# Block 0's down product of a fused attention and SwiGLU kernel: another order for three VectorE sums, for the sums of x and for two groups of basis work

## The chip, the cores and the metric

The kernel runs on one core of one Trainium2 chip. The metric is the device time of one execution in microseconds (us). Its time before is 1006.44 us, the median of three runs (1006.27 to 1007.7). All times below are us unless they are marked ns.

A core has a matrix engine (TensorE, PE in the profile; its weight loads are PEld), a vector engine (VectorE, DVE), a scalar engine (ScalarE, ACT), a general one (GpSimd, POOL), and SyncE (SP), which here only issues DMAs. Each engine works its own queue in order, and they meet at semaphores. SBUF is the working memory; PSUM, in banks, is where matmuls leave their results.

## The reference

```python
kv  = einsum('bhsd,bhse->bhde', k, v)           # 8 batches, 8 heads, 576 positions, head size 64
o   = einsum('bhsd,bhde->bhse', q, kv)
x   = o / sqrt(mean(o * o, -1) + 1e-6) * g_norm # reshaped to 4608 x 512
g   = x @ w_gate                                # 512 x 1536
out = (g * sigmoid(g) * (x @ w_val)) @ w_out    # 1536 x 512
```

Everything is float32 in the kernel; the weights arrive as 64-bit words and are rounded on the chip.

## The kernel before, in words

**Tiling.** The 4608 rows are nine blocks of 512. Each goes through attention (class `Att`: x of the block, transposed), an *up* product (`Up`, `Inner`: h = silu(x w_gate) * (x w_val), in six pairs of 128-wide columns) and a *down* product (`Down`: h w_out). Block 0's up is a plain product (`plain_up`); blocks 1 and 2 and all downs but the last use one level of a seven-product scheme for 2 x 2 blocks (Strassen's, in Winograd's form); the last six blocks go in pairs, with two levels in their ups. While a block is in its down, the next block's attention is worked in between.

**The seven products.** P1 to P7 are each a chain of matmuls. `CHAIN` (line 634) gives each a bank of PSUM: P1, P6, P7 and P4 add up in one bank "b"; P2 has a bank "a"; P5 opens a bank "c", and P3 adds on top of it. After some products the result is taken out, or partly summed, by ACT or DVE: `after1`, `after6`, `after2`, `after7`, `after4`, `after3`. The operands need sums: S1 to S4 of the left side, T sums of the weights (the *basis*: `t2` and the subtractions in `Up.prepare` and `turn_t`).

**Block 0's down.** `Ffn.down` (line 1453) goes through P1, P6, P5, P7, P2, P4, P3, 24 matmuls each. Named here:

- `after7` (line 1380) copies bank b on ACT (U3) and then adds bank c, P5, to it on DVE. This sum is `added`. P3 is written into the same bank c, so P3 waits until `added` has read it.
- `after2` (line 1374) adds bank a, P2, to the copy of P1 on DVE (here "the sum with P2"), and then computes S4 on DVE, 128 x 1536, in place of an operand of P2. P3 reads S4.
- `after4` and `after3` finish the two halves of the block's output, which SP stores.

**Block 1's attention beside it.** `Att.steps` (line 601) hands three steps to block 0's down: the products of q with kv, norms and transposes after P1 (`whole`), the transposed blocks' DMAs after P5 (`place_x`: 16 DMAs, eight of them issued on ACT's queue, eight on SP's), and after P2 the gain on ACT (`gain_x`) and the four sums of x on DVE (`sums`, `sum_steps`). Block 1's P5 reads the first of these sums, P6 the third.

**Basis work.** In lines 1711 to 1716 `t2` (line 1574) makes, on DVE, two instructions for each of six pairs of w_val's columns. The first three pairs are queued behind block 1's scaled x (`nxt.halves[0]`), the other three behind S4 and `added`. POOL subtracts from what `t2` leaves (`Up.prepare`, line 693).

**The kept leaves.** For blocks 3 to 8 the weights are also turned into the second level's 49 combinations ("leaves"), written to DRAM by SP (`send_leaf`), and streamed back later. `kept_steps(0)` (line 1304) is the work for pair 0 in two halves, each of four DVE instructions (three of 128 x 256, one of 128 x 512) and two DMAs; four raw DMAs follow. The first half is placed by hand in `alone` (line 1636) ahead of block 0's down. The second half is handed to block 1's up, in `Up.multiply` (line 748): its first instruction, `held`, is queued behind block 1's scaled x (`ffn.att.scaled`), for pair 1 behind `ffn.added`, the sum of P5 and U3 of block 1's pair 0. SP's sends keep the program's order. The halves for pair 0 and pair 1 use the same room in SBUF, so pair 1's second half waits until pair 0's second half has been sent.

**What sets the order.** The kernel is written in a framework that sets all semaphores itself and orders each engine's queue by its own reckoning of when things are ready. `tc.issue_after(ins)` is the hand's way in: whatever the block under it issues on the engine of `ins` comes behind `ins` in that engine's queue. `in_order` fixes a whole stretch; it is not used around the change. In block 0's down DVE's queue before had, after x's scaling and transposes: `t2` of pairs 0 to 2 with the four instructions of the kept half among them, the sum with P2, S4, `added`, then `t2` of pairs 3 to 5 with x's sums among them.

Of the kernel before, what the change touches and what calls it, by code (L numbers as in the profile page):

```python
# [18 lines left out]
def kernel(  # L19
# [41 lines left out]
    nc = tc.nc  # L61
# [5 lines left out]
    BLK = P * T  # L67
    HB = BLK // 2
    HD = DM // 2
# [61 lines left out]
    add = lambda e, o, a, b: e.tensor_tensor(out=o, in0=a, in1=b, op=OP.add)  # L131
    sub = lambda e, o, a, b: e.tensor_tensor(out=o, in0=a, in1=b, op=OP.subtract)  # L132
# [24 lines left out]
    def ring():  # L157

        return r_pool.tile([P, 4, BLK], F32, name="r")
# [75 lines left out]
    class Att:  # L235
# [300 lines left out]
        def sums(self):  # L536

            for step in self.sum_steps():
                step()

        def sum_steps(self):

# [54 lines left out]
        def turn(self):  # L597
            for i in range(2):
                self.turn_q(i, (c_psum if self.n == 1 else m_psum, b_psum))
# [45 lines left out]
    class Quad:  # L645
# [9 lines left out]
        def multiply(self, p):  # L655
            name, first = CHAIN[p]
            if first:
                self.ps[name] = PSUMS[name].tile([P, 2, HB], F32, name=name)
            ps = self.ps[name]
            for e, i in self.order(p):  # L660
                lhsT, rhs = self.operands(p, e, i)

                self.ffn.multiplied = nc.tensor.matmul(  # L663
                    ps[:, e], lhsT=lhsT, rhs=rhs, start=first and i == 0 and e == 0, stop=i == self.steps - 1,
                    skip_group_check=True,
                )
            getattr(self, f"after{p}", lambda: None)()
# [17 lines left out]
    class Up(Quad):  # L685
# [24 lines left out]
        def after2(self):  # L710
            add(nc.vector, self.s, self.ps["a"], self.s)
            if self.j == NP - 1:
                nc.scalar.activation(out=self.s, in_=self.s, func=ACT.Silu)
# [34 lines left out]
        def multiply(self, p):  # L748
            super().multiply(p)
            ffn = self.ffn  # L750
            if ffn.n == 1:
                if p == 5:
                    self.leaf_room = chunks(ring())
                if p in (5, 7, 4):
                    at = 3 * (5, 7, 4).index(p)
                    ffn.making.extend(leaf_steps(self.j, [(self.w[p].unsqueeze(1), (p,))], self.leaf_room[:, at:]))
                if p == 3:
                    if self.j < 2:
                        first, *steps = first_kept if self.j == 0 else kept_steps(self.j, chunks(xi_alone))

                        def held():
                            with tc.issue_after((ffn.added if self.j else ffn.att.scaled).ins):
                                first()

                        ffn.later += [held, *steps]
# [503 lines left out]
    def leaf_steps(j, sources, room):  # L1269


        i = 0
        for t, os in sources:
            n = len(os)
            t = t.rearrange("p o i (e c) -> p o i e c", e=2)
            b11, t2_, b22 = t[:, :, 0, 0], t[:, :, 0, 1], t[:, :, 1, 1]
            to = room[:, i : i + 3 * n].rearrange("p (o r) c -> p o r c", r=3)
            yield lambda b22=b22, t2_=t2_: sub(nc.vector, t2_, b22, t2_)
            yield lambda b11=b11, t2_=t2_: add(nc.vector, t2_, t2_, b11)
            yield lambda t=t, t2_=t2_, to=to, n=n: sub(  # L1280
                nc.vector, to[:, :, 1:3], t[:, :, 1], t2_.unsqueeze(2).to_broadcast([P, n, 2, P])
            )
            yield lambda t=t, os=os: send_leaf(j, os, (1, 6, 2, 3), t.rearrange("p o i e c -> p o (i e c)"))
            yield lambda b11=b11, t2_=t2_, to=to: sub(nc.vector, to[:, :, 0], b11, t2_)
            yield lambda to=to, os=os: send_leaf(j, os, (7, 4, 5), to.rearrange("p o r c -> p o (r c)"))
            i += 3 * n
# [13 lines left out]
    def chunks(t):  # L1300

        return t.rearrange("p f (s c) -> p (f s) c", c=P) if len(t.shape) == 3 else t.rearrange("p a b c -> p (a b) c")
# [21 lines left out]
    class Down(Quad):  # L1324
# [47 lines left out]
            sub(nc.vector, pairs[:, 0, :, 0:HB], pairs[:, 0, :, HB:BLK], pairs[:, 1, :, HB:BLK])  # L1372

        def after2(self):
            add(nc.vector, self.o1[:, :, 0:HD], self.ps["a"], self.s)

            pairs = self.ffn.h.rearrange("p (j e) t -> p e j t", e=2)
            self.s4 = sub(nc.vector, pairs[:, 1, :, 0:HB], pairs[:, 1, :, 0:HB], pairs[:, 0, :, HB:BLK])

        def after7(self):  # L1380
            o = ring()
# [185 lines left out]
    def weights(upto):  # L1567
        nonlocal rounded
        while rounded < min(upto, len(pieces)):
            load_weights(rounded + 4)  # L1570
            round_w(*pieces[rounded])
            rounded += 1

    def t2(place, b22, b11):

        sub(nc.vector, place, b22, place)
        return add(nc.vector, place, place, b11)
# [58 lines left out]
    def alone(n):  # L1636
        ffn = Ffn(n, blocks[n])
        nxt = blocks[n + 1]
        if n == 0:

            with tc.issue_after(squared.ins), tc.issue_after(scaled.ins):
                weights(2)
            ffn.plain_up(0, (0,))
            copied = blocks[0].copied
            blocks[0].turn_x(1)
            for f in range(NF - 1):
                with tc.issue_after(blocks[0].copied.ins if f else copied.ins):
                    weights(2 * (f + 2))
                ffn.plain_up(f) if f else ffn.plain_up(0, (1,))
            weights(len(pieces))  # L1650
            pairs = wo.rearrange("p (j e) d -> p e j d", e=2)
            turned = t2(pairs[:, 0, :, HD:DM], pairs[:, 1, :, HD:DM], pairs[:, 0, :, 0:HD])
            nxt.room = xi_alone.rearrange("p a b c -> p (a b c)")

            with tc.issue_after(sent.ins):
                for i in range(2):
                    nxt.load_kv(i)
                nxt.load_quarters(0)
            with tc.issue_after(ffn.silus[NF - 2].ins):
                for step in nxt.quarter_steps(1, (0, 1), (nc.scalar,)):  # L1660
                    step()
            with tc.issue_after(turned.ins):
                nxt.turn_q(0)
            with tc.issue_after(nxt.q_turned.ins):
                multiplied = ffn.plain_up(NF - 1)
            with tc.issue_after(multiplied.ins):
                nxt.turn_q(1)
            ffn.s1 = s_pool.tile([P, NP, HB], F32, name="s1")
            ffn.plain_end()
            for g in range(2):  # L1670
                nxt.kv(g)
            with in_order(nc.vector.engine), tc.issue_after(nxt.q_turned.ins):
                one, two = ffn.sum_steps()
                one()
                for _ in range(6):
                    first_kept.pop(0)()
                two()
        elif n == 1:

            def third():  # L1680
                visit(ffn, nxt, (0, 1))
                for i in range(2):
                    nxt.load_q(i)

            ffn.up({(1, 7): third})
            nxt.turn()
            blocks[PAIRED].load_kv(0)
        else:
            with in_order(nc.vector.engine, nc.scalar.engine):
                ffn.up(ahead(ffn, nxt, blocks[PAIRED + 1]))  # L1690
            nxt = blocks[PAIRED + 1]
            nxt.turn()
            for g in range(2):
                blocks[PAIRED + 2].load_kv(g)
        if n == 2:
            ffn.down_.opens = PAIRED

        def inner_sums():
            with tc.issue_after(nxt.scaled.ins):
                blocks[PAIRED].inner_sums()  # L1700

        def second_kv():
            with tc.issue_after(nxt.placed.ins):
                blocks[PAIRED].load_kv(1)

        ffn.down(nxt, {1: {5: second_kv}, 2: {7: inner_sums}}.get(n, {}))
        if n == 0:
            for g in range(2):
                blocks[2].load_kv(g)

            with tc.issue_after(nxt.halves[0].ins):
                for j in range(NP // 2):
                    t2(wv[j][:, 0:2], wv[j][:, 2:4], wg[j][:, 0:2])
            with tc.issue_after(ffn.down_.s4.ins), tc.issue_after(ffn.down_.added.ins):
                for j in range(NP // 2, NP):
                    t2(wv[j][:, 0:2], wv[j][:, 2:4], wg[j][:, 0:2])

    first_kept = list(kept_steps(0, chunks(xi_alone)))
    for n in range(PAIRED):
        with in_order(nc.tensor.engine) if n == 2 else ExitStack():  # L1720
            alone(n)
# [65 lines left out]
```

## Time and profile before

| what | value |
|---|---|
| median of three runs | 1006.44 (1006.27, 1006.44, 1007.7) |
| the profiled execution | 1004.65 |
| its span, first to last instruction | 1002.8 |
| TensorE's granted clock, mean | 0.999 |
| TensorE busy | 986.6 (98%) |
| VectorE busy | 714.0 (71%) |
| GpSimd busy | 408.8 (41%) |
| ScalarE busy | 231.3 (23%) |
| block 0's down on TensorE, P1 to P3 | 115.7 to 156.1 of the span |
| block 1's up on TensorE | 156.0 to about 231 |

The profile is of one execution. A row of the timeline or of the chain gives the start in us from the span's start, the length, the engine, the line of the kernel (a helper's line where a helper records the instruction: L131, L132 and L133 are `add`, `sub` and `mul`, L663 is the matmul of `Quad.multiply`), the tile written and those read (r, wo, arena, t lie in SBUF; a, b, c, m are PSUM), the partitions and elements, and, in brackets, how long the engine was idle before it and what ended that. Matmuls overlap, and their ends are modelled, so starts are the safer reading. A wait list gives who waited for whom: the total, how often, the longest.

### The profile page before, as it was taken

Reading aid. Unit: us, or ns where it says so; the run is one execution under the profiler, and the core shown is the slowest. Engines: PE = TensorE matmul, PEld = TensorE weight load, DVE = VectorE, ACT = ScalarE, POOL = GpSimd, SP = SyncE. Lnnn points to the kernel's source line nnn. Section 1 sums busy time; section 2 is a strip of 40 time slices with the busy share of each in tenths; the row PEclk is TensorE's granted clock in tenths of the full one; section 3 lists DMA queues with packets and bytes.
Section 4 is the critical chain, followed back from the end, with each engine's and each line's share of the span. In section 5 each row is a group of like instructions: output and inputs, shape, how many; then the busy total and the mean of one; then the engine's idle time right before and its main releaser. Section 6 shows DMA issues by size and latency. Waiting matters only on the chain.

```text
span 1002.8 us, 17762 instructions
## 1 busy us (share of the span) xinstructions
PE 986.6 (98%) x6758; PEld 833.9 (83%) x6758; DVE 714.0 (71%) x1171; ACT 231.3 (23%) x367; POOL 408.8 (41%) x328
## 2 busy tenths in 40 slices
PE   6999999999999999999999999999999999999998
PEld 4544688888888888888888888888888888888998
DVE  2999697678858576656675846666776576666894
ACT  2766111221122312121211111122112112122100
POOL 0000263355544240444566003555651078999300
PEclk9999999999999999999999999999999999999999
DMA  8689743573866855766752365667412556565123
GB/s 230 200 265 265 154 74 119 123 260 95 211 135 127 208 112 167 186 185 169 171 151 43 99 158 149 159 178 179 111 19 67 119 169 204 182 212 161 48 84 96
DMA packets 268261, 151.54 MB, mean 151 GB/s; under 512 B 150288, under 2 KB 250128, under 8 KB 268176
## 3 DMA queue, kind: packets, MB, share of 16 engines
q1 hardware_dynamic: 230928, 144.89, 53.0%
q10 hardware_dynamic: 37184, 5.51, 3.2%
q8 instruction: 54, 0.88, 0.4%
q14 instruction: 31, 0.25, 0.1%
q0 software_dynamic: 64, 0.00, 0.0%
HBM read 109.12 MB, written 32.83 MB: 142 GB/s over the span
## 4 chain that ended last, share of the span: by engine, by line
PE 94%; DVE 3%; DMA 1%; ACT 1%; issue 0%; SPq 0%; DVEq 0%; ACTq 0%
PE b L826 22%; PE b L663 21%; PE c L663 11%; PE c L826 11%; PE a L826 5%; PE a L663 5%; PE b L1489 4%; PE c L1489 4%; PE b L905 4%; PE c L905 2%; PE m L436 1%; PE m L375 1%; DVE arena L132 1%; PE a L905 1%; DMA arena<-in_v_dram 1%; DVE arena L131 0%
## 5 line engine op out<-in xcount | busy, mean ns | idle before, releaser
L826 PE MATMUL b<-arena,t 128*128 128x256 f32 x1008 | 244.5, 381 | 0.0
L826 PEld LDWEIGHTS b<-arena,t 128*128 128x128 f32 x1008 | 190.0, 190 | 29.4 <-DVE r L131 2.3
L131 DVE TENSOR_TENSOR r<-b,r 128x512 f32<-128x512 f32 (+1 forms) x248 | 146.0, 601 | 67.5 <-PE b L826 54.9
L131 POOL TENSOR_TENSOR r<-r 128x256 f32<-128x256 f32 (+1 forms) x90 | 94.8, 1056 | 168.0 <-DMA t<-w 93.3
L131 DVE TENSOR_TENSOR r<-c,r 128x512 f32<-128x512 f32 (+1 forms) x171 | 105.6, 625 | 58.1 <-PE c L826 40.0
L133 POOL TENSOR_TENSOR arena<-r 128x1024 f32<-128x1024 f32 (+1 forms) x54 | 101.7, 1899 | 92.9 <-DVE r L131 49.1
L131 DVE TENSOR_TENSOR r<-a,r 128x512 f32<-128x512 f32 x95 | 60.3, 635 | 100.3 <-PE a L663 64.0
L132 POOL TENSOR_TENSOR t<-wo 128x512 f32<-128x512 f32 x45 | 64.1, 1445 | 162.7 <-DVE wo L131 102.9
L132 DVE TENSOR_TENSOR arena<-arena 128x512 f32<-128x512 f32 (+4 forms) x117 | 123.1, 1069 | 10.2 <-PE b L663 7.0
L826 PE MATMUL c<-arena,t 128*128 128x256 f32 x504 | 122.5, 379 | 0.0
L826 PEld LDWEIGHTS c<-arena,t 128*128 128x128 f32 x504 | 95.6, 190 | 13.5 <-DVE r L131 0.3
L663 PE MATMUL b<-wo,arena 128*128 128x256 f32 x336 | 76.4, 382 | 0.1
L840 ACT COPY r<-b 128x512 f32<-128x512 f32 x54 | 31.7, 586 | 190.0 <-PE b L826 190.0
L663 PE MATMUL b<-t,arena 128*128 128x256 f32 x336 | 74.8, 379 | 0.0
L132 POOL TENSOR_TENSOR t<-arena 128x512 f32<-128x512 f32 x36 | 51.9, 1456 | 55.1 <-PE c L663 21.4
L663 PEld LDWEIGHTS b<-t,arena 128*128 128x128 f32 x336 | 63.8, 190 | 8.7
L663 PEld LDWEIGHTS b<-wo,arena 128*128 128x128 f32 x336 | 63.1, 190 | 9.6 <-DVE arena L133 0.9
L826 PE MATMUL a<-arena,t 128*128 128x256 f32 x252 | 66.1, 379 | 0.0
L826 PEld LDWEIGHTS a<-arena,t 128*128 128x128 f32 x252 | 47.9, 190 | 6.5
L663 PE MATMUL b<-arena 128*128 128x256 f32 x192 | 45.5, 380 | 0.0
L663 PE MATMUL b<-arena,t 128*128 128x256 f32 x192 | 45.4, 379 | 0.0
L1489 PE MATMUL b<-arena 128*128 128x512 f32 (+1 forms) x104 | 43.5, 561 | 0.6 <-ACT arena L500 0.6
(142 smaller groups left out, 1408.2 us busy)
## 6 DMA issues: line engine op xcount, KB each, us to landing
t<-w SPq DMA_DIRECT2D x180, 256.0 KB, 3.2
ld<-in_k_dram SPq DMA_DIRECT2D x26, 288.0 KB, 4.4
ld<-in_v_dram SPq DMA_DIRECT2D x26, 288.0 KB, 6.0
out_dram<-r SPq DMA_DIRECT2D x14, 512.0 KB, 3.2
t<-w SPq DMA_DIRECT2D x54, 128.0 KB, 2.7
ld<-in_moe_w_gate_dram SPq DMA_DIRECT2D x12, 512.0 KB, 4.7
ld<-in_moe_w_val_dram SPq DMA_DIRECT2D x12, 512.0 KB, 4.5
ld<-in_moe_w_out_dram SPq DMA_DIRECT2D x12, 512.0 KB, 4.7
```

The lines of the kernel that those rows point to most:

```text
L131: add = lambda e, o, a, b: e.tensor_tensor(out=o, in0=a, in1=b, op=OP.add)
L132: sub = lambda e, o, a, b: e.tensor_tensor(out=o, in0=a, in1=b, op=OP.subtract)
L133: mul = lambda e, o, a, b: e.tensor_tensor(out=o, in0=a, in1=b, op=OP.mult)
L375: self.positions = nc.tensor.matmul(self.kv_ps[r][u * D : (u + 1) * D, g, :], lhsT=k[:, u, c, :], rhs=v[:, u, c, :], start=(c == 0), stop= ...
L436: self.multiplied = nc.tensor.matmul(self.ps[i][u][p : p + D, t, j, :], lhsT=self.qt[rows, tile_t, head, p : p + D], rhs=kvs[b % 3][rows, ...
L663: self.ffn.multiplied = nc.tensor.matmul(ps[:, e], lhsT=lhsT, rhs=rhs, start=first and i == 0 and e == 0, stop=i == self.steps - 1, skip_g ...
L826: self.ffn.multiplied = nc.tensor.matmul(ps[:, i], lhsT=stream.use(self.ffn.n, self.j, o, p), rhs=self.operand(o, p), start=first and i == ...
L840: copied = nc.scalar.copy(out=dst, in_=ps)
L905: self.ffn.multiplied = nc.tensor.matmul(ps[:, i, f], lhsT=self.deep.operand(o, p, c)[:, f], rhs=self.deep.weight(o, p, c, f), start=first ...
L1489: nc.tensor.matmul(t, lhsT=w[f // 2][:, i, P * (f % 2) : P * (f % 2 + 1)], rhs=x[:, i, of], start=(i == 0), stop=(i == NS - 1),)
```

## The change

Three edits, all to the order of queues; no instruction is added or taken away.

1. `after2`, in block 0 alone: S4 is queued behind `added`, and the sum with P2 behind S4. Before, and still in the other blocks, the sum with P2 is issued first and S4 second, with no order to `added`.
2. `Up.multiply`: the second half of `kept_steps(0)` is queued behind `ffn.added` (as pair 1's already was), no longer behind block 1's scaled x.
3. `alone`: `t2` of pairs 3 to 5 is queued behind S4 and the last of x's sums (`sums` now keeps it as `last_sum`), no longer behind S4 and `added`.

```diff
@@ Att.sums
             for step in self.sum_steps():
-                step()
+                self.last_sum = step()
@@ Up.multiply
                         def held():
-                            with tc.issue_after((ffn.added if self.j else ffn.att.scaled).ins):
+                            with tc.issue_after(ffn.added.ins):
                                 first()
@@ Down.after2
-            add(nc.vector, self.o1[:, :, 0:HD], self.ps["a"], self.s)
-
             pairs = self.ffn.h.rearrange("p (j e) t -> p e j t", e=2)
-            self.s4 = sub(nc.vector, pairs[:, 1, :, 0:HB], pairs[:, 1, :, 0:HB], pairs[:, 0, :, HB:BLK])
+
+            def turn():
+                self.s4 = sub(nc.vector, pairs[:, 1, :, 0:HB], pairs[:, 1, :, 0:HB], pairs[:, 0, :, HB:BLK])
+
+            def total():
+                return add(nc.vector, self.o1[:, :, 0:HD], self.ps["a"], self.s)
+
+            if self.ffn.n == 0:
+                with tc.issue_after(self.added.ins):
+                    turn()
+                with tc.issue_after(self.s4.ins):
+                    total()
+            else:
+                total()
+                turn()
@@ alone
-            with tc.issue_after(ffn.down_.s4.ins), tc.issue_after(ffn.down_.added.ins):
+            with tc.issue_after(ffn.down_.s4.ins), tc.issue_after(nxt.last_sum.ins):
                 for j in range(NP // 2, NP):
                     t2(wv[j][:, 0:2], wv[j][:, 2:4], wg[j][:, 0:2])
```

## The prediction

> **What bounds the kernel now.** I read the page's busy times first, then all waits of TensorE, then its timeline around the change, then the chain there, and last the queues of DVE, ACT, POOL and SP.
>
> ```profile
> PE 986.6 (98%) x6758; PEld 833.9 (83%) x6758; DVE 714.0 (71%) x1171; ACT 231.3 (23%) x367; POOL 408.8 (41%) x328
> ```
>
> TensorE works 98% of the span, so only its idle time can be won. From 36 us to the end the list of its waits has one entry over a tenth of a microsecond:
>
> ```profile
> PE c L663 <- DVE r L131: 1.4, 1, 1.4
> ```
>
> It lies in block 0's down, in the timeline of TensorE:
>
> ```profile
> 133.59 5.34 PE L663 MATMUL b<-t,arena 128*128 128x256 f32 x24
> 138.77 5.34 PE L663 MATMUL a<-wo,arena 128*128 128x256 f32 x24
> 143.95 5.34 PE L663 MATMUL b<-t,arena 128*128 128x256 f32 x24
> 150.66 5.45 PE L663 MATMUL c<-wo,arena 128*128 128x256 f32 x24 [1.37 <-DVE r L131]
> 155.95 0.38 PE L663 MATMUL b<-arena 128*128 128x256 f32 x1
> ```
>
> The rows are P7, P2, P4, P3 and the first matmul of block 1's up. P3 goes onto the bank c that holds P5, so it needs `added` (the sum that reads P5), and S4 for its operand. The chain names what made `added` late:
>
> ```profile
> 141.09 3.09 DVE arena L131 x2
> 144.18 0.02 issue
> 144.20 3.06 DVE arena L132 x2
> 147.26 0.60 DVE r L131
> 147.87 2.14 DVE arena L132
> 150.01 0.61 DVE r L131
> ```
>
> The last three are the sum with P2, S4, and `added`. `added` ran last, though its other input, the copy of U3 on ACT, was there at 142.4:
>
> ```profile
> 141.80 0.59 ACT L1384 COPY r<-b 128x512 f32<-128x512 f32 x1 [12.17 <-DMA arena<-r]
> ```
>
> **The change part by part**
>
> **`added` first, then S4, then the sum with P2.** Nothing is added or removed; three DVE instructions change places. DVE is in order, so behind `added` wait S4, the sum, x's sums and three pairs' basis. `added` can run from 142.4 to 143.1 (0.68 by its row). S4 overwrites an operand of P2, which ends at 144.1. It is 128x1536. It took 2.22 in place (147.79), and the same form 1.75 at 125.33 with POOL idle. The highest bound, three times the longest 128x512 beside POOL (1.75), is 5.25. So S4 ends between 145.9 and 149.4; I take 2.22, the row of S4 itself: 146.4. Without a wait P3 starts at 143.95 + 5.18 = 149.13 (5.18 is the distance of P7, P2 and P4). Only the highest bound makes P3 wait, 0.27. P1 of block 1 would start at 149.13 + 5.18 = 154.31, where it now starts at 155.95: **a gain of 1.64** (1.53 from P3's start, 0.11 from the resumed pass, whose successor comes 5.29 after it instead of 5.18). By the bounds of S4: 1.64 - 0.27 = 1.37 to 1.64.
>
> The Trainium skill ("SBUF — State Buffer", section "SBUF: two separate sides") speaks against moving S4 here: a DVE instruction with two SBUF inputs and a GpSimd one share a port pair that one holds for a whole instruction, while the other blocks. POOL runs basis subtractions from 137.57 to 152.80, and rows agree: 128x256 takes 0.42 at 118.07 and 1.49 at 139.60, beside POOL. By the rule S4 waits for one POOL instruction (1.27 alone) and then runs its 1.75, 3.0 in all, ending at 147.1, in time; by its own row at 146.4. Both leave the gain at 1.64.
>
> **The sum with P2 later.** From about 146.4 to 147.1, or 150.1 at the highest bound. It frees bank a, next needed by P2 of block 1's first pair (161.13 now, 159.5 then). That cover is over 9 us; gone, it would cost one for one.
>
> **x's sums ahead of three pairs' basis (`t2`, j of 3 to 5).** Four instructions overtake six. `gain_x` ends on ACT at 146.15, so the sums can start right behind the sum with P2. The first to need one is P5 of block 1's first pair, at 154.31 + 1.73 = 156.0 (1.73 is what eight matmuls take in the chain); it reads the first sum. P6, at 157.8, reads the third. At the longest row, 1.75 each, from the latest start, 150.1, the first ends by 151.9, the third by 155.4, and the fourth by 157.1, before anything reads it. The basis is read by POOL's subtractions for pair 3, the first of which runs at 162.56 and waits for a DMA. So nothing here is on the path; I count 0, from 0 to 0.
>
> **The second half of `kept_steps(0)` moves into block 1's up.** This is the second hunk, and the part with a price. Its four DVE instructions now run at 139.60, 142.69, 144.20 and 145.78, and take 1.41 + 1.51 + 2.99 = 5.9 of DVE's time there:
>
> ```profile
> 145.78 1.49 DVE L132 TENSOR_TENSOR arena<-arena 128x256 f32<-128x256 f32 x1
> ```
>
> The other half, the same four forms at 118.07 with POOL idle, took 1.94 in all. Taken out, they let `t2` of pairs 0 to 2 end by about 141, before U3's copy. Put behind the `added` of block 1's pair 0 (165.62 now, 163.98 then), they delay DVE by 1.94 to 5.9. I take 1.94, since POOL has one subtraction there (167.28, then 165.6). Their four DMAs sit on SP behind the leaf sends and ahead of the next sends:
>
> ```profile
> 173.77 0.32 SPq L1267 DMA_DIRECT2D w<-r  x1
> 174.14 2.11 SPq L1267 DMA_DIRECT2D w<-arena  x4
> ```
>
> Their place on SP is fixed, but they go only after DVE's leaf work, which the set now delays. DVE waits for their landing:
>
> ```profile
> 173.67 0.68 DVE L131 TENSOR_TENSOR r<-c,r 128x512 f32<-128x512 f32 x1
> 176.16 1.04 DVE L132 TENSOR_TENSOR arena<-arena 128x256 f32<-128x256 f32 x1 [1.82 <-DMA w<-arena]
> ...
> 180.43 0.68 DVE L131 TENSOR_TENSOR r<-c,r 128x512 f32<-128x512 f32 x1
> ```
>
> The last row is `added` of pair 1, which frees bank c for P3 of pair 1 (184.30; with the gain 182.66). DVE from 166.3 to 174.3 is full, so nothing absorbs the delay. The sum then ends at 181.11 - 1.64 + 1.94 = 181.4, and P3 still has 1.2 of cover. With 5.9 it ends at 185.4 and P3 waits 2.7. I take no stall.
>
> **The sum.** 1.64 + 0 + 0 - 0 = 1.64 less; at the worst ends of both unknown costs 1.37 - 2.7, that is 1.3 more. The profiled execution has a span of 1002.8 and took 1004.65, 1.85 around the span; it becomes 1001.2 and 1003.0. The median shown, 1006.44, is 1.79 above that execution; the same 1.64 off it gives **1004.8**.
>
> **What is late next.** Nothing on TensorE: the rest of the way to the end the only other gap that I find is 0.12 long, near 310 us, so a gain beyond about 1.76 has no place to come from.
>
> **The rivals**
>
> *The moved set eats the gain.* For it: DVE is nearly full from 164 to 174, and the set's sends gate the next basis set. Against: 1.2 of cover, and little POOL work there. A delay of 3.2 to 5.9 takes 0 to 2.7 back, so 1004.8 to 1007.5; at the bound of 5.9, **1007.5**.
>
> *Slower: DVE stands at the landing of the moved sends ahead of pair 1's sum, and P3 of pair 1 waits on bank c.* To be 0.2% slower (2.0; about what a measurement of this kernel can tell from no change) P3 must wait 2.0 + 1.64 = 3.65, so the sum must end past 186.3, 6.8 later behind TensorE than now. That is past the 5.9, so it takes the set at its dearest and 0.9 more from a second collision with POOL (rows of 1.27), or a place in DVE's queue behind further leaf steps. Speaking for it is that the order of block 1's queues is chosen anew once these edges differ, and only bank c's 3.2 of cover (184.30 - 181.11) stands in the way. Against it: no P3 of block 1 waits today. Two such stalls, in pairs 1 and 2, of 3.7 each give 1006.44 - 1.64 + 7.4 = **1012**, one gives **1008.5**.
>
> *The change doesn't do what it says.* `added` still comes late, because U3's copy on ACT stands behind sixteen transfers' issues (eight on ACT: 134.35, 7.40 long) and slips behind `gain_x`, at 146.15. Then the copy (0.59) ends at 146.7, `added` at 147.4, S4 at 149.6, and P3 waits 0.5, which gives 1005.3; with an S4 of 3.25, inside its bounds, P3 starts as late as now, at 150.65: **1006.4**.
>
> **How the numbers follow.** Forecast 0.66 at 1004.8; gain eaten 0.16; slower 0.13; not done 0.05. The three runs lie 1.4 apart, so I give the forecast 0.8 either side: 1004.0 to 1005.6. The range goes up to 1007.6 to take in the second case and the fourth; left out are the slower case and 0.05 of scatter. Faster by over 0.2% means below 1004.43, which the mechanism can't reach from the median; scatter can, with 0.20 taken out of the forecast's 0.66. The rest of it, the second and the fourth case are within 0.2%: 0.67. Slower is 0.13.
>
> **What would show it.** On DVE after the six `t2` instructions: the sum into r from c at about 142.4, then 128x1536 at 144.1, then the sum from a. TensorE's wait list has no entry for P3 of block 0, whose row starts at 149.1, and block 1's first matmul at 154.3. Four instructions of 128x256 and 128x512 are gone from 139 to 147 and follow the sum from c at about 164. Wrong would be: a new wait "PE c <- DVE r" between 165 and 200, DVE idle for over 3 us on "DMA w<-arena", or P3 waiting on "DVE arena" (S4) in place of "DVE r".

## The result, and the profile after

The median after is 1004.12 us (8 runs, 1002.36 to 1005.17), beside 1006.62 for the kernel before (8 runs, 1005.67 to 1007.7). The ratio is 0.9974, 95% interval 0.9963 to 0.9984. Two repetitions on two chips, below, gave 0.9984 (0.9976 to 0.9993) and 0.9981 (0.9972 to 0.9990). So the change is faster, by some 0.2%, and the predicted 1.64 us (0.9984 of 1006.44) lies in all three intervals, in the first one at its edge.

The profiled execution took 1004.81 with a span of 1003.0: by its span alone nothing was won, for before had 1002.8. From the page after:

```profile
span 1003.0 us, 17761 instructions
PE 986.4 (98%) x6758; PEld 834.1 (83%) x6758; DVE 711.7 (71%) x1171; ACT 231.3 (23%) x367; POOL 408.7 (41%) x328
```

The first row that is free of the start-up's waits is the first matmul of block 0's up that isn't interrupted again. Its row before, and after, from the timelines of TensorE:

```profile
34.26 1.99 PE L1489 MATMUL b<-arena 128*128 128x256 f32 x8 [0.21 <-ACT arena L500]
```

```profile
35.66 1.99 PE L1501 MATMUL b<-arena 128*128 128x256 f32 x8 [0.22 <-ACT arena L500]
```

Already here the execution after is 1.40 late: TensorE's waits for the first loads came out longer in it (10.8 in all, 9.4 before). Times after are therefore read against this row. TensorE around block 0's down, after (P7, P2, P4, P3, then block 1's first product):

```profile
134.98 5.34 PE L663 MATMUL b<-t,arena 128*128 128x256 f32 x24
140.16 5.34 PE L663 MATMUL a<-wo,arena 128*128 128x256 f32 x24
145.34 5.34 PE L663 MATMUL b<-t,arena 128*128 128x256 f32 x24
150.52 5.34 PE L663 MATMUL c<-wo,arena 128*128 128x256 f32 x24
155.70 0.59 PE L663 MATMUL b<-arena 128*128 128x256 f32 x2
```

P3 follows P4 by 5.18, with no wait. From the row above to block 1's first product (called the distance from here on) it is 155.70 - 35.66 = 120.04; before it was 155.95 - 34.26 = 121.69. The difference, 1.65, is the gain. DVE's timeline after shows why:

```profile
139.33 1.75 DVE L132 TENSOR_TENSOR arena<-arena 128x512 f32<-128x512 f32 x1
141.12 1.64 DVE L131 TENSOR_TENSOR arena<-arena 128x512 f32<-128x512 f32 x1
143.73 0.69 DVE L131 TENSOR_TENSOR r<-c,r 128x512 f32<-128x512 f32 x1 [0.97 <-ACT r L1396]
145.54 2.42 DVE L132 TENSOR_TENSOR arena<-arena 128x1536 f32<-128x1536 f32 x1 [1.12 <-PE a L663]
147.89 0.68 DVE L131 TENSOR_TENSOR r<-a,r 128x512 f32<-128x512 f32 x1
```

The first two rows are the end of `t2` of pairs 0 to 2; DVE then is idle twice, for U3's copy and for the end of P2, and `added`, S4 and the sum with P2 follow, all done at 148.6, two ahead of P3's start. The wait list of TensorE from 36 us on has other entries now:

```profile
PE b L375 <- DMA ld<-in_v_dram: 0.6, 1, 0.6
PE b L1501 <- ACT arena L500: 0.2, 1, 0.2
```

The first is the gap near 310 us that was 0.12 before. It eats some of the gain in this execution, and it varies: 0.6, 0.9, 0.5 and 0.8 in the four profiles of the first question below, 0.9 in the third one of the changed kernel. Together with the start-up's 1.40 it is why the spans say nothing.

### The profile page after: what moved, and what is told of

Read it like the earlier page. It is cut to its first block, busy times and chain, and to the rows that moved or that the text cites. A ratio compares the mean times of both kernels' runs of the same rounds, so it can differ in the third digit from the quotient of the medians.

```text
span 1003.0 us, 17761 instructions
## 1 busy us (share of the span) xinstructions
PE 986.4 (98%) x6758; PEld 834.1 (83%) x6758; DVE 711.7 (71%) x1171; ACT 231.3 (23%) x367; POOL 408.7 (41%) x328
## 4 chain that ended last, share of the span: by engine, by line
PE 95%; DMA 2%; ACT 1%; DVE 1%; SPq 0%; POOL 0%; issue 0%; DVEq 0%; POOLq 0%; ACTq 0%
PE b L663 22%; PE b L826 22%; PE c L663 11%; PE c L826 11%; PE a L663 6%; PE a L826 5%; PE b L1501 4%; PE c L1501 4%; PE b L905 4%; PE c L905 2%; PE m L436 1%; PE m L375 1%; DMA arena<-in_v_dram 1%; PE a L905 1%; DMA ld<-in_v_dram 1%; DMA arena<-in_k_dram 0%
```

## The experiments

**First question: which part of the change does it?** My theory was that DVE comes late because of the work ahead of all three sums; the rival that their order counts, as the change says. Each part was put alone into the kernel before. The whole change ran beside them.

The whole change again (the same kernel):

> The changed kernel once more, timed beside the three parts of it. Theory (P3's wait is all of it): 1.64 us less than the kernel before, a ratio of 0.9984, and in a profile the starts of the matmuls before P3 and after it shift against the kernel before by 1.64. Rival (something besides P3's wait was won, since the two medians lie 2.5 apart): about 2.5 less again, 0.9975, and a second step in the shift of the matmuls' starts, toward earlier, that comes back in every profile.

Measured: 1004.10 beside 1005.88, a ratio to the kernel before of 0.9984 (0.9976 to 0.9993). The profile's distance is 155.09 - 35.04 = 120.05, again 1.64 less. There is no second step toward earlier: what differs from the kernel before elsewhere are waits for DMAs that vary (the gap at 310, and 0.3 on a leaf's load at 504). The excess of the first comparison did not come back here or in the third one below; I take it for scatter.

The order alone (part of its diff):

```diff
+            if self.ffn.n == 0:
+                with tc.issue_after(self.added.ins):
+                    turn()
+                with tc.issue_after(self.s4.ins):
+                    total()
```

> Only the new order of the three sums (the sum that takes P5, then S4, then the sum with P2); the kept half stays among the first basis work, and the other basis work waits as before. Theory A (DVE is late because of the work ahead of all three, not because of their order): the kept half still ends at 147.2 in the old profile's time, the sum with P5 at 147.9, S4 at 150.1, so P3 starts at 150.1 to 150.2 instead of 150.66, now waiting for S4: 0.5 us less than before. Theory B (the order is what counts, as the change says): P3 without a wait, 1.6 less.

Measured: a ratio of 0.9997 (0.9988 to 1.0006); the distance is 156.22 - 35.13 = 121.09, 0.60 less than before. Its timeline of TensorE, P3's row:

```profile
150.94 5.45 PE L663 MATMUL c<-wo,arena 128*128 128x256 f32 x24 [0.78 <-DVE arena L132]
```

and of DVE:

```profile
145.07 3.06 DVE L132 TENSOR_TENSOR arena<-arena 128x512 f32<-128x512 f32 x2
148.06 0.68 DVE L131 TENSOR_TENSOR r<-c,r 128x512 f32<-128x512 f32 x1
148.66 2.22 DVE L132 TENSOR_TENSOR arena<-arena 128x1536 f32<-128x1536 f32 x1
```

The kept half (the last two of it are the first row) still ends at 148.1; P3 now waits for S4 instead of for `added`. The new order saves what the sum with P2 took ahead of S4, 0.60 from start to start, and no more.

The kept half alone:

```diff
-                            with tc.issue_after((ffn.added if self.j else ffn.att.scaled).ins):
+                            with tc.issue_after(ffn.added.ins):
```

> Only the kept half moved into block 1's up; the order of the three sums stays the old one (sum with P2, S4, sum with P5). Theory A: the basis work ends at about 141, the sum with P2 runs at 144.1, S4 to 147.2, the sum with P5 to 147.9, still ahead of the end of P4 at 149.1, so P3 doesn't wait and the kernel takes 1.6 us less, as much as the whole change. Theory B: the sum with P5 still comes last and P3 waits nearly as long as before: 0 to 0.3 less.

Measured: 0.9986 (0.9977 to 0.9994), as the whole change. The distance is 155.35 - 35.17 = 120.18, 1.51 less; 0.1 of the difference to 1.64 was lost before block 0's down. Its timelines of DVE and of TensorE:

```profile
145.19 0.69 DVE L131 TENSOR_TENSOR r<-a,r 128x512 f32<-128x512 f32 x1 [2.79 <-PE a L663]
145.80 1.81 DVE L132 TENSOR_TENSOR arena<-arena 128x1536 f32<-128x1536 f32 x1
147.53 0.68 DVE L131 TENSOR_TENSOR r<-c,r 128x512 f32<-128x512 f32 x1
```

```profile
144.99 5.34 PE L663 MATMUL b<-t,arena 128*128 128x256 f32 x24
150.17 5.34 PE L663 MATMUL c<-wo,arena 128*128 128x256 f32 x24
```

With the old order, `added` still last, and all is done at 148.2, two ahead of P3. DVE waits 2.79 for P2: it isn't late any more, so its order is free. In the times the intervals of this run and of the order alone overlap; it is the distances, 1.51 and 0.60 less, that tell them apart.

x's sums ahead of three pairs' basis alone (the hunk in `alone`; `last_sum` is kept as in the change):

```diff
-            with tc.issue_after(ffn.down_.s4.ins), tc.issue_after(ffn.down_.added.ins):
+            with tc.issue_after(ffn.down_.s4.ins), tc.issue_after(nxt.last_sum.ins):
```

> Only x's sums ahead of three pairs' basis. Both theories: nothing on TensorE's path, P3 waits 1.4 as before, the same time as before (within 0.3 us in the profile's shift of the matmuls). Rival (the excess of 0.9 over P3's wait comes from here): 0.5 to 0.9 less, with an earlier start of block 1's P5 or P6 against P1.

Measured: 1.0002 (0.9993 to 1.0010), a distance of 156.84 - 35.14 = 121.70, P3 waiting 1.4 as before. Nothing is seen of it by itself.

**Second question: is a wait of TensorE paid one for one?** Additions were put on DVE between `added` and S4, into a place that the sum with P2 overwrites:

```diff
+                last = self.added
+                for _ in range(8):
+                    with tc.issue_after(last.ins):
+                        last = add(nc.vector, self.o1[:, :, 0:HD], self.s, self.s)
-                with tc.issue_after(self.added.ins):
+                with tc.issue_after(last.ins):
                     turn()
```

> The changed kernel with eight more 128x512 additions on DVE between the sum that takes P5 and S4 (they write a place that the sum with P2 overwrites later). x's sums fall among them. Theory (a delay of P3 past the end of P4 is paid one for one, and nothing behind it catches up): beside POOL an addition takes about 1.5, alone 0.6; twelve instructions from 144.4 on end between 153 and 157, S4 by 155 to 159, so P3 starts 5 to 8 later than in the changed kernel, and the whole is longer by what P3's row shows, within 0.3 in the profile. Rival (block 1's up has slack that takes up a late start): the matmuls' shift shrinks again later in the trace, and the time is under half of P3's delay longer.

Measured: 1.0030 (1.0020 to 1.0040). The changed kernel was not timed beside it; against its two repetitions' ratios this is some 4.6 to 4.9 us more. This one missed: the framework answered the late S4 by putting three products of block 1 (P1, P5, P6) ahead of P3 in TensorE's queue. P3 started 8.9 later, but TensorE waited only 1.5 for P6's operand and 1.9 for S4. So it could not tell one for one from anything. With four additions (the same diff with `range(4)`) TensorE's order holds:

> As the run with eight additions before S4, but four, with which TensorE's queue keeps its order (with eight, three products of block 1 stood ahead of P3). From the row of the earlier run (four took 6.2 beside POOL): the sum that takes P5 ends at 144.4 in the changed kernel's time, the additions at 150.6, S4 (1.75 to 2.4) at 152.4 to 153.0, so P3 starts 1.8 to 2.5 later than at 150.52. Theory (one for one): P1 of block 1 starts 1.9 to 2.6 later, and so does every product up to the wait for v at 310, which shrinks by what it is (0.6): in the times 1.3 to 2.6 more than the changed kernel. Rival (slack behind it takes it up): the delay is smaller by block 1's pair 1 already.

Measured: 1.0027 (1.0016 to 1.0037), 4.4 us more than the changed kernel beside it (1008.73 to 1004.34), where 1.3 to 2.6 were expected. P3's row, and its successor, from TensorE's timeline:

```profile
152.42 7.13 PE L663 MATMUL c<-wo,arena 128*128 128x256 f32 x24 [2.80 <-DVE arena L132]
159.40 1.89 PE L663 MATMUL b<-arena 128*128 128x256 f32 x8
```

The wait was 2.80 (the four additions took 6.40 and S4 2.81, beside POOL), but the pass after it took 7.13 instead of 5.34. Block 1's first product came at 159.40 - 34.59 = 124.81, 4.77 later than in the changed kernel. The table by stretches gives the granted clock (the column behind POOL's):

```profile
149.00:152.40 3.40, 0.62 (x3) 0.19 (x2) 3.40 (x3) 0.58 (x1) 3.40 (x3) 1.00 0.36 139
152.40:154.00 1.60, 1.58 (x6) 1.33 (x7) 1.60 (x3) 0.00 (x0) 1.10 (x1) 0.76 0.09 33
154.00:156.00 2.00, 2.00 (x6) 1.64 (x5) 1.93 (x4) 0.00 (x0) 0.00 (x0) 0.50 0.00 0
156.00:157.50 1.50, 1.50 (x7) 1.22 (x7) 1.50 (x4) 0.00 (x0) 0.00 (x0) 0.79 0.00 0
157.50:161.00 3.50, 3.50 (x18) 3.09 (x17) 2.90 (x5) 0.00 (x0) 0.00 (x0) 1.00 0.02 5
```

The means of 0.76 and 0.79 say that the clock went to 0.50 about 0.8 after P3 had started, stayed there for about 3.4 and came back. Neither one for one nor slack: P3 started 2.97 later than in the changed kernel, and its pass cost 1.80 more. Before, with a wait of 1.37, the pass took 5.45, and the clock stayed at 1.00:

```profile
149.00:150.60 1.60, 0.29 (x2) 0.00 (x0) 1.60 (x3) 0.59 (x1) 1.60 (x1) 1.00 0.00 0
150.60:152.00 1.40, 1.34 (x6) 1.21 (x7) 1.40 (x3) 0.00 (x0) 1.40 (x2) 1.00 0.30 114
```

**Third question: is bank c of block 1's pair 1 the place where the moved half would hurt, and with how much cover?** First as a load on DVE, sixteen repeats of the half's first instruction:

```diff
                                 first()
+                                if self.j == 0:
+                                    for _ in range(16):
+                                        first()
```

> The changed kernel with the first instruction of the moved half (128x256, 0.41 alone) repeated sixteen times on DVE in block 1's up, ahead of the sum of P5 and U3 of pair 1. In the changed kernel's profile that sum ends at 181.5 and P3 of pair 1 starts at 184.06: 2.5 of cover. Theory (the prediction's price for the moved half: P3 of pair 1 waits when DVE falls behind by more than the cover): 16 x 0.41 = 6.6, a few collisions with POOL more, so a wait of 4 to 6 on TensorE between 183 and 192 and 4 to 6 us more than the changed kernel, that is 2.4 to 4.4 more than the kernel before. Rival (DVE's idle 1.8 at the landing of the sends, and later idle time, take it up): 0 to 2.3 more than the changed kernel and no such wait in the list, or one under 2.3.

Measured: 1.0005 (0.9996 to 1.0014), by the same reckoning 2.1 to 2.4 more than the changed kernel, but no wait in pair 1. DVE's timeline, the sum that frees bank c, and TensorE's, the P3 that needs it:

```profile
180.68 0.68 DVE L131 TENSOR_TENSOR r<-c,r 128x512 f32<-128x512 f32 x1
```

```profile
182.50 1.89 PE L663 MATMUL c<-arena 128*128 128x256 f32 x8
```

The theory's wait did not come in pair 1: the framework put pair 1's half, which waits for the sends, behind this sum (DVE stands at them for 1.08 at 185.38; in the changed kernel for 1.84 at 176.94, ahead of the sum). What was paid stands elsewhere in its wait list: 0.3 on the same kind of sum, for P3 of block 1's last pair at 228.25, 0.8 on a product of POOL at 235.40, and twice 0.5 on leaf loads at 504 and 507 (0.3 of the latter kind came without the load, too). The rival's number was right, its reason only in part. So the load was put where it can't be passed by, eight additions right ahead of that sum (part of the diff; elsewhere the sum stays as it was):

```diff
+            if self.ffn.n == 1 and self.j == 1:
+                g = self.piece(3)
+                for _ in range(8):
+                    last = add(nc.vector, g, self.u3, self.u3)
+                with tc.issue_after(last.ins):
+                    added = add(nc.vector, self.u3, self.ps["c"], self.u3)
```

> The changed kernel with eight 128x512 additions on DVE right ahead of the sum of P5 and U3 of block 1's pair 1 (into a place that is written later). TensorE's order is the changed kernel's. In that kernel the sum ends at 181.5, P3 of pair 1 starts at 184.06. Theory (2.5 of cover, then one for one): 8 x 0.6 = 4.8 put its end at 186.3, so TensorE waits 2.3 on it, up to 3.5 with one collision with POOL, and the kernel takes 1.7 to 3.5 more than the changed kernel (0.6 of it may go into the wait for v at 310). Rival (as in the run with sixteen repeats, bank c is no bound there): no wait between 183 and 187, the same time.

Measured: 1.0054 (1.0039 to 1.0070), 6.4 more than the changed kernel. TensorE's timeline from P3 of pair 1:

```profile
186.96 3.78 PE L663 MATMUL c<-arena 128*128 128x256 f32 x8 [4.21 <-DVE r L131]
190.54 2.85 PE L663 MATMUL b<-arena 128*128 128x256 f32 x8
193.23 1.89 PE L663 MATMUL a<-arena 128*128 128x256 f32 x8
```

The additions took 6.8 (179.39 to 186.22), not 4.8; 6.8 less the cover of 2.5 is 4.3, against a wait of 4.21. The place and its cover are right. Then the clock again: two passes took 3.78 and 2.85 instead of 1.89. The table by stretches has

```profile
182.70:187.00 4.30, 0.09 (x2) 0.04 (x1) 4.13 (x7) 0.60 (x1) 0.03 (x1) 0.84 0.32 51
189.00:191.00 2.00, 2.00 (x7) 1.53 (x6) 1.90 (x8) 0.00 (x0) 0.00 (x0) 0.50 0.39 62
191.00:193.00 2.00, 2.00 (x7) 1.66 (x6) 0.62 (x2) 0.00 (x0) 1.26 (x1) 0.63 0.41 66
```

By the mean of 0.84 the clock fell before the wait was over; by that of 0.63 it was back at about 192.5. Against the changed kernel the third row is (193.23 - 34.19) - (187.51 - 35.66) = 7.2 late: 4.4 of wait and 2.8 of clock.

**Fourth: what is late next.** TensorE's wait for v at 310 was taken away by turning to that work one product later:

```diff
-            (3, 1): lambda: half(1), (4, 1): att.place_x, ...
+            (3, 5): lambda: half(1), (4, 1): att.place_x, ...
```

> The changed kernel with what is late next taken away: in block 2's up, TensorE goes to the second half of block 4's k and v one product later (behind P5 of pair 3 instead of P1), 1.73 later, since its wait for the landing of v is 0.5 to 0.9 in five profiles out of six. Theory: that wait is gone and nothing takes its place, 0.5 to 0.9 less than the changed kernel, so 2.1 to 2.5 less than the kernel before, a ratio of 0.9975 to 0.9979, and a shift of the matmuls at 310 by as much. Rival (the steps of that attention come later and block 3's rows, placed by DMA, turn late instead): a new wait on TensorE behind 310 and no gain on the changed kernel, 0.9984.

Measured: 0.9973 (0.9964 to 0.9982). The wait list has no entry at 310, and one of 0.2 for a leaf load that the changed kernel's lists don't have. Since that is no more than the first comparison gave for the changed kernel alone, it was repeated beside the changed kernel:

> The changed kernel beside the next one on the same chip. 1.64 less than the kernel before, 0.9984, as in the repetition.

> The changed kernel with the later turn to block 4's k and v, again, beside the changed kernel. Theory: 0.5 to 0.9 less than the changed kernel, a ratio to the kernel before of 0.9975 to 0.9979, the wait for v gone from the list. Rival: what the wait cost comes back at later waits for DMAs (0.2 at 427 in the first run), and the two agree within 0.3.

Measured: 0.9981 (0.9972 to 0.9990) for the changed kernel, with the distance 155.05 - 35.00 = 120.05 and a wait of 0.9 for v; 0.9982 (0.9973 to 0.9990) with the later turn, whose wait list from 36 us on is empty. In the profile TensorE is idle 0.9 less, in the times the two agree. Whether it beats the changed kernel stays open; at most it is worth the 0.5 to 0.9, and the intervals are about 0.9 to either side.

## Why the prediction was right, point by point

- **The bound.** Right: the one wait was P3's, and with it gone the distance on TensorE shrank by 1.64 to 1.65 in all three profiles of the changed kernel.
- **`added`, S4, the sum with P2.** Right in each time: 1.40 off the profile after, `added` starts at 142.3, S4 at 144.1, the sum with P2 at 146.5, against 142.4, 144.1 and 146.4. S4 took 2.42, against 2.22. In the rows shown S4 took 1.81 (the kept half alone) to 2.81 (four additions), within the 1.75 to 3.0 that the rule of the shared port pair gives. Two slips of the working change nothing: the row at 118.07 is 0.41 (0.42 is the next one), and 144.1 + 2.22 is 146.3.
- **To whom the gain was credited.** Here the prediction was wrong in its account, not in its sum. It booked 1.64 under the new order, and took the kept half for "the part with a price", at 0 here. The runs book it the other way: the kept half alone gives 1.51 (0.9986), the order alone 0.60 (0.9997), and the order adds nothing measurable once the half is gone (1004.10 for both together, 1004.19 for the half alone). What made `added` late was the work ahead of all three sums. The working held the reason ("Taken out, they let `t2` of pairs 0 to 2 end by about 141") but did not ask what each edit gives without the other.
- **x's sums ahead.** Right: 0 was booked, and alone they gave 1.0002.
- **The moved half in block 1's up.** It went where it was expected, behind the sum at 165.37; less the 1.40 that is 163.97, against 163.98. No stall, right. But the cover left was 2.5, not 1.2: the sum of pair 1 came 0.7 later behind TensorE, not 1.94. In DVE's timeline the moved instructions stand mixed with those around them, and one of 128x128 (181.79) now comes behind that sum; how much each of these gave was not tried. That the outcome was right here doesn't rest on the 1.94.
- **The rivals.** None came. The slower one had the right place (bank c of pair 1) and a price that was too low: it took a wait of 3.7 for 3.7, and the runs put 7.2 on one of 4.2.
- **What is late next.** "The only other gap that I find is 0.12" was one execution's; in most others it is 0.4 to 0.9, and the runs with eight additions before S4 and with sixteen repeats have no entry for it. With x's sums alone, where nothing was won ahead of it, it is 0.8, so it isn't the change that makes it. It doesn't change the sum, but it can hide a third or more of the gain in one profile.
- **The range and the chances.** 1004.12 is in the range, near its lower end. Whether the change is over or under 0.2% can't be told: 0.26% in the first comparison, 0.16% and 0.19% in the next two, each about 0.09% to either side.

## What to carry to other kernels

When an instruction comes late, look first at what stands ahead of the whole group in its queue: work that is ready early and needed late. Moving that out made the order inside the group not matter, while the order alone moved the wait from one operand to the other and took 0.60 off it. Edits that come together should be costed one without the other, and two executions should be compared from the first row behind the start-up, product by product, not by their spans.

## What the runs showed of the hardware that I had not expected

P3's wait of 1.37 was paid about one for one (its removal gave 1.64: 1.53 from P3's start and 0.11 from the pass behind it), at a granted clock of 1.00. In the run with eight additions waits of 1.52 and 1.85 left the clock at 1.00, too. One of 2.80 was followed by a clock of 0.50 for about 3.4 and put the next product 4.8 later (4.4 in the times); one of 4.21 kept it at half until about 192.5 and put the third row 7.2 later (6.4 in the times). The Trainium skill ("TensorE: Matmul & The Clock Gate", section "Part 1: The HAM clock gate (the "warmup" mystery)") says that the clock is halved after at least one idle window of about 3.4; here 2.80 was enough, and the measurement decides. Why it was enough stays open.

DVE instructions with both inputs in SBUF ran much longer while POOL was at work: four 128x512 additions took 6.40 in the run with four, 1.6 each, where in the run with eight single ones took 0.60 from start to start once POOL had nothing left to do. S4 took 2.81 in the first of these runs and 1.74 in the second.
